# A chunked recurrence and a feed-forward block on one core: another fixed order of the first part, and four units whose scores come from the split form

## The chip, the cores and the metric

The kernel runs on one core of one Trainium2 chip. The metric is the device time of one execution in microseconds (us). The kernel before was run three times: 340.52, 343.04 and 342.12 us, a median of 342.12 us.

## The reference, cut to what matters

Four sequences of 768 tokens and 8 heads go through a linear recurrence, computed in chunks of 32 tokens. Its output (3072 tokens by 256) goes through a feed-forward block of width 2048 with a softplus between two matrix products. All of it is float32.

```python
log_a = np.log(np.clip(a, 1e-06, 1.0))
for c in range(nc):
    cum = np.cumsum(la, axis=-1)
    L = np.exp(cum[:, :, :, None] - cum[:, :, None, :]) * causal
    M = np.einsum('bhin,bhjn->bhij', Cc, Bc) * L
    y[:, :, sl] = (np.einsum('bhij,bhjd->bhid', M, xc)
                   + np.einsum('bhin,bhnd->bhid', Cc, state) * np.exp(cum)[:, :, :, None])
    state = decay_full * state + np.sum(Bx, axis=2)
...
h = x @ w_in
g = np.maximum(h, 0.0) + np.log1p(np.exp(-np.abs(h)))
out = g @ w_out
```

## The kernel before, in words

The recurrence is cut into 24 units of 128 tokens by 8 heads, six units for each sequence. Unit `i` goes through these steps (the letter in brackets is its word in the order):

- `decays` (D, L340): one affine select on POOL spreads the decay factors into `rm`, 128x1024.
- `score` (S, L378): the products of B and C, two 128x512 tiles `sp`, one for each group of four heads. There are two forms. A unit below `FIRST` (L30) is loaded with 576 KB from the array `fst`, in which C already lies apart by heads, and each tile is one plain float32 product over 64 rows (L386; L127 for units 0 to 7). A unit from `FIRST` on is loaded with 768 KB from the array `un`, and its tiles are four fp32r products of 256 columns (L391). These need `split_unit` first (L238): for `c_all` and for `b_rows` one copy on ACT (L247) and one scalar_tensor_tensor on DVE (L248), and two DMAs that put the halves of `c_all` into `c_rows` (L254). `c_rows` exists once, so one unit's DMAs wait until the scores of the unit before are done.
- `weigh` (M): two DVE products `m<-sp,rm`. `scale_b` (B) and `scale_c` (C) scale B and C by decays.
- `update` (U): products `zp` on PE, then `state` on DVE. `spread` (T) and `read` (R) bring the state before into `yp`; `within` (I) adds the unit's own 16 products.
- `grow` (G): two DVE products `y<-yp,gg`, one for each group of heads, then a copy to `xh` on ACT; `rest` (X): `xl<-y,xh` on DVE. `xh` and `xl` are the high and low parts of the block's input. `gg` is loaded from DRAM by `load_growth` (L225), 2 DMAs for three units (so `gg6` serves units 6 and 7).

The feed-forward block works on six pieces `j` of 512 tokens and 16 slices `k` of its width. `first` (F j.k) is six products `hp` of 512 columns (three for each half of the 256 inputs: high by high, low by high, high by low). `parts_of` (P) is a softplus `e` and a cast `gh` on ACT and a subtraction `gl` on DVE. `second` (Z j.k) is six products into two accumulators: `acc<-gh,woh`, `acc<-gl,woh`, `acc<-gh,wol` for each. The weights come in 16 loads (w0 to w15, 512 KB each, four buffers `wraw`) and are taken apart by `split_stages` (W, L522): one op on ACT, a shift and two scalar_tensor_tensor `w<-wraw,w` on DVE, a cast on ACT, and the subtraction `wil` or `wol` on DVE. Even steps make `wih`/`wil`, odd steps `woh`/`wol`. The fourth stage of a W is the last that reads its `wraw`, so the load that takes this buffer next waits for it.

**What sets the order.** All loads are issued on SP, one after the other, and each waits there until its buffer is free; the loads behind it wait too. For the first part (units 0 to 7, slices 0.0 to 0.11 and 1.0 to 1.7) the string `ORDER` (L53 to L68) lists every step by hand, and each engine keeps to it; these instructions all have the line L127 in the profile. A word of a staged step stands once for each of its stages: of W1 (stage 4 is the second scalar_tensor_tensor), of G6 (stage 1 is the two `y`), of P0.3 (stage 3 is `gl`). `warm` words put unused products on PE. What comes behind (units 8 to 23, the rest of the block, L761 on) is placed by a scheduler; unit 8's values go in at step `U_STEP[0]` = 20, and `prefetch` loads unit `i + 2` one step after unit `i`'s scores.

Of the kernel before, what the change touches and what calls it, by code (L numbers as in the profile page):

```python
# [26 lines left out]
NFT = DFF // P  # L27
TOK = NB * S
HEAD = 4
FIRST = 12  # L30
GU = 3
U_X = 0
U_B = U_X + DM
# [17 lines left out]


ORDER = """  # L53
warm1 warm7 la kc hc0 kb un0 w0 loga hc1 loga un1 gb ft0 lr hc2 un2 fr0 ft0 S0 w2 fr0 hc3 D0 fr0 un3 gq0 un4
fr0 w1 D1 W0 gq2 M0 w4 gq0 fr2 M0 S1 gq2 D3 fr2 C1 I0 logr M1 ft2 logr B0 B1 growth U0 C2 U1 U0 W0 fr2
growth T1 B2 fr2 gd U1 ft2 U2 M1 un5 D2 U2 R1 W2 G0 S3 G0 C3 W0 S2 T3 M3 I1 warm3 T2 W0 w6 M2 W0 M3 R3 D4 M2
I3 G1 R2 S4 G1 X0 C4 W0 gg3 I2 warm2 X1 W4 B3 D5 M4 G2 H0 C5 M4 U3 H1 W2 G2 U3 W2 S5 warm4 X2 T4 W2 w3 G3 W2
B4 R4 un6 M5 G3 I4 W2 U4 D6 G4 W1 U4 H2 G4 M5 H3 X3 X4 F0.0 T5 W4 F0.1 W1 P0.0 W4 R5 P0.1 W1 F0.2 P0.0 W4 I5
P0.1 w5 W1 F0.3 W4 D7 w7 G5 S6 warm2 W1 un7 G5 gg6 P0.2 W4 X5 W6 F0.4 M6 P0.2 W6 M6 F0.5 P0.0 W1 P0.3 I6 W6
W3 Z0.0 B6 P0.3 W6 w8 P0.1 U6 W6 U6 C7 Z0.1 W3 W6 P0.4 G6 S7 W5 T7 W3 G6 P0.2 R7 P0.4 F0.6 X6 P0.5 M7 P0.5  # L60
W3 F0.7 w10 M7 W3 P0.3 I7 W3 P0.6 G7 W7 Z0.2 W5 G7 P0.4 X7 P0.7 Z0.3 W5 P0.6 P0.5 W5 P0.7 F1.0 w12 W7 W5
P0.6 F1.1 P1.0 W5 W7 W8 Z0.4 P0.7 P1.1 W7 P1.0 F1.2 w14 W8 B7 W7 W8 W7 Z0.5 P1.2 P1.0 W10 W8 F1.3 P1.1 w9
W10 W8 P1.1 Z0.6 W8 P1.3 W10 W14 F1.4 P1.2 W10 w11 P1.2 W10 Z0.7 W14 P1.4 W10 W14 W9 F1.5 P1.3 W9 W14 F1.6
P1.5 w13 P1.3 W14 W9 F1.7 P1.6 W14 W9 W11 F0.8 w15 W11 W9 W11 F0.9 W9 W11 W13 F0.10 K0 W13 W13 W11 F0.11 W13
W11 W13 Z1.0 W15 W13 W15 W12 U7 Z1.1 W15 P1.4 W12 P1.4 P1.5 Z1.2 W12 P1.7 P1.5 P1.6 W15 Z1.3 P0.9 P1.6 W15
W12 P1.7 Z1.4 U7 W15 P0.11 P1.7 W12 Z1.5 P0.9 W12 P0.10 P0.9 P0.11 Z1.6 P0.8 P0.11 P0.10 Z1.7 P0.10 P0.8 K1
P0.8 zero
"""  # L68
HALF = NFT // 2
AHEAD = 20  # L70
# [34 lines left out]
def recurrence_then_ffn(ctx: ExitStack, tc: tile.TileContext, fst, un, at, al, w_in, w_out, const, outT):  # L105
# [28 lines left out]
    def load(out, in_):  # L134

        tc.keep_in_program_order(nc.sync.dma_start(out, in_))  # L136
# [73 lines left out]
    def load_unit(i):  # L210
# [4 lines left out]
        un_s[i] = p3.tile([P, U_END], F32, tag="un", name=f"un{i}")  # L215
        if i < FIRST:
            load(un_s[i][:, :F_END], fst[i])
        else:
            load(un_s[i], un[i - FIRST])

# [17 lines left out]
    def split_unit(i):  # L238
        if i < FIRST:
            return  # L240
        t = un_s[i]
        b_rows = p2.tile([P, NQ, P], F32R, tag="b_rows", name=f"b_rows{i}")

        def split(out, j):
            raw = t[:, U_S + j * NQ * P : U_S + (j + 1) * NQ * P].rearrange("p (q t) -> p q t", q=NQ)
            g, be = (kb[:, C_GB + v : C_GB + v + 1] for v in (2 * j, 2 * j + 1))
            A.activation(out, raw, AF.Copy, scale=be)  # L247
            V.scalar_tensor_tensor(out, raw, g, out.bitcast(F32), op0=ALU.mult, op1=ALU.add)  # L248

        c_all = p2.tile([P, NQ, P], F32R, tag="c_all", name=f"c_all{i}")  # L250
        split(c_all, 1)
        for e in range(2):
            rows = slice(64 * e, 64 * e + 64)
            load(c_rows[rows, :, e].bitcast(F32), c_all[rows].bitcast(F32))  # L254
        split(b_rows, 0)
        st[i] = b_rows
# [121 lines left out]
    def score(i, g):  # L378
        sp = mid[i]["sp", g] = ps.tile([P, 512], F32, tag="ps", name=f"sp{i}_{g}")
        if i < FIRST:  # L380
            rows = slice(64 * g, 64 * g + 64)
# [452 lines left out]
```

## Time and profile before

| | |
|---|---|
| three runs | 340.52, 343.04, 342.12 us (median 342.12) |
| profiled execution | 340.56 us, of which the span of the profile is 338.8 us |
| busy, share of the span | PE 328.7 us (97%), DVE 202.8 (60%), ACT 171.7 (51%), POOL 39.3 (12%) |
| TensorE clock granted | full speed in all 40 slices |
| DMA | 35.01 MB, mean 103 GB/s |

A row of the page's fifth part, or of the view by lines, names line, engine, operation, output and inputs, the count, busy time and the mean ns of one, and the idle time of its engine just before with what ended it. The chain of waits gives start, length, engine and product of each piece of the chain that ended last. In a timeline, an entry gives start, length, engine, line, operation and, in brackets, how long the engine stood idle before it and for what. The sixth part of the page gives the KB of each DMA and the time from issue to landing.

### The profile page before, as it was taken

Reading aid. Unit: us, or ns where it says so; the run is one execution under the profiler, and the core shown is the slowest. Engines: PE = TensorE matmul, PEld = TensorE weight load, DVE = VectorE, ACT = ScalarE, POOL = GpSimd, SP = SyncE. Lnnn points to the kernel's source line nnn. Section 1 sums busy time; section 2 is a strip of 40 time slices with the busy share of each in tenths; the row PEclk is TensorE's granted clock in tenths of the full one; section 3 lists DMA queues with packets and bytes.
Section 4 is the critical chain, followed back from the end, with each engine's and each line's share of the span. In section 5 each row is a group of like instructions: output and inputs, shape, how many; then the busy total and the mean of one; then the engine's idle time right before and its main releaser. Section 6 shows DMA issues by size and latency. Waiting matters only on the chain.

```text
span 338.8 us, 5271 instructions
## 1 busy us (share of the span) xinstructions
PE 328.7 (97%) x2047; PEld 249.4 (74%) x2047; DVE 202.8 (60%) x394; ACT 171.7 (51%) x319; POOL 39.3 (12%) x32
## 2 busy tenths in 40 slices
PE   8789998999999999999999999999999999999995
PEld 4446657887666678778778778778778778888885
DVE  0899989996946444864765464777474342232242
ACT  4845666875715435445445455445445244444450
POOL 2434510000111010110112010111010000000000
PEclk9999999999999999999999999999999999999999
DMA  7964533573032205416434205443203100010001
GB/s 233 396 228 138 220 106 104 188 259 120 3 98 114 93 0 189 133 39 186 126 61 141 95 0 188 122 106 99 94 2 93 33 0 0 2 55 8 2 0 62
DMA packets 19376, 35.01 MB, mean 103 GB/s; under 512 B 1432, under 2 KB 10136, under 8 KB 19352
## 3 DMA queue, kind: packets, MB, share of 16 engines
q1 hardware_dynamic: 19352, 34.68, 31.5%
q8 instruction: 16, 0.26, 0.3%
q14 instruction: 8, 0.07, 0.1%
HBM read 28.28 MB, written 3.24 MB: 93 GB/s over the span
## 4 chain that ended last, share of the span: by engine, by line
PE 86%; DVE 6%; DMA 5%; SPq 1%; issue 1%; ACT 0%
PE hp L563 32%; PE acc L642 32%; PE hp L127 6%; PE acc L127 6%; PE yp L466 3%; DMA gg<-gd 3%; DMA head_in_l<-in_fst 2%; PE yp L450 2%; PE sp L391 2%; DVE m L127 1%; DVE w L127 1%; PE sp L386 1%; SPq L136 1%; PE zp L416 1%; PE end L127 1%
## 5 line engine op out<-in xcount | busy, mean ns | idle before, releaser
L603 DVE TENSOR_TENSOR gl<-e,gh 128x512 fp32r<-128x512 f32 x76 | 55.7, 734 | 61.3 <-ACT gh L597 61.1
L597 ACT CAST gh<-e 128x512 fp32r<-128x512 f32 x76 | 47.1, 620 | 61.1 <-PE acc L642 60.3
L591 ACT ACTIVATE e<-hp 128x512 f32<-128x512 f32 x76 | 45.1, 596 | 42.4 <-DVE gl L603 38.5
L563 PE MATMUL hp<-xh,wih 128*128 128x512 f32 x152 | 61.3, 405 | 0.0
L642 PE MATMUL acc<-gl,woh 128*128 128x512 f32 x155 | 60.6, 391 | 0.0
L642 PE MATMUL acc<-gh,wol 128*128 128x512 f32 x155 | 60.5, 391 | 0.0
L642 PE MATMUL acc<-gh,woh 128*128 128x512 f32 x155 | 59.6, 391 | 0.0
L563 PE MATMUL hp<-xl,wih 128*128 128x512 f32 x152 | 59.5, 392 | 0.0
L563 PE MATMUL hp<-xh,wil 128*128 128x512 f32 x152 | 59.3, 391 | 0.0
L345 POOL TENSOR_SCALAR_AFFINE_SELECT rm<-fc 128x1024 f32<-128x1024 f32 x16 | 23.8, 1487 | 187.7 <-DVE m L402 167.8
L563 PEld LDWEIGHTS hp<-xh,wih 128*128 128x128 f32 x152 | 28.5, 188 | 10.7 <-issue 3.1
L642 PEld LDWEIGHTS acc<-gh,woh 128*128 128x128 f32 x155 | 29.1, 188 | 6.8 <-issue 0.8
L642 PEld LDWEIGHTS acc<-gh,wol 128*128 128x128 f32 x155 | 29.1, 188 | 6.2
L642 PEld LDWEIGHTS acc<-gl,woh 128*128 128x128 f32 x155 | 29.1, 188 | 6.1 <-issue 0.2
L563 PEld LDWEIGHTS hp<-xh,wil 128*128 128x128 f32 x152 | 28.5, 188 | 6.3
L563 PEld LDWEIGHTS hp<-xl,wih 128*128 128x128 f32 x152 | 28.6, 188 | 5.1
L402 DVE TENSOR_TENSOR m<-sp,rm 128x512 f32<-128x512 f32 x32 | 20.9, 685 | 7.9 <-PE sp L391 6.3
L127 DVE SCALAR_TENSOR_TENSOR w<-wraw,w 128x512 int32<-128x512 int32 x32 | 23.1, 729 | 0.2
L127 PE MATMUL hp<-xh,wih 128*128 128x512 f32 (+1 forms) x48 | 17.7, 368 | 2.0 <-DVE m L127 1.4
L127 PE MATMUL hp<-xl,wih 128*128 128x512 f32 (+1 forms) x48 | 17.0, 354 | 0.0
L127 PE MATMUL hp<-xh,wil 128*128 128x512 f32 (+1 forms) x48 | 17.0, 354 | 0.0
L127 POOL TENSOR_SCALAR_AFFINE_SELECT rm<-fc 128x1024 f32<-128x1024 f32 x8 | 14.0, 1764 | 20.8 <-DVE m L127 15.0
(109 smaller groups left out, 409.6 us busy)
## 6 DMA issues: line engine op xcount, KB each, us to landing
un<-in_un SPq DMA_DIRECT2D x12, 768.0 KB, 4.4
un<-in_fst SPq DMA_DIRECT2D x8, 576.0 KB, 6.1
wraw<-in_w_in SPq DMA_DIRECT2D x8, 512.0 KB, 3.4
wraw<-in_w_out SPq DMA_DIRECT2D x8, 512.0 KB, 5.2
c_rows<-c_all SPq DMA_DIRECT2D x24, 128.0 KB, 2.4
out_t<-o SPq DMA_DIRECT2D x11, 256.0 KB
gg<-gd SPq DMA_DIRECT2D x14, 192.0 KB
head_in_l<-in_fst SPq DMA_DIRECT2D x4, 320.0 KB, 6.2
```

What stands on the lines that cost most here:

```text
L127: return lambda *a, **k: tc.keep_in_program_order(f(*a, **k))
L136: tc.keep_in_program_order(nc.sync.dma_start(out, in_))
L345: Pl.affine_select(out=rm.rearrange("p h c i -> p (h c) i"), in_=fc[:, u].rearrange("p h c -> p (h c)").unsqueeze(2).broadcast_to([P, NH * ...
L391: PE.matmul(sp[:, 2 * v * P : 2 * (v + 1) * P], b_rows[:, q], c_rows[:, q].rearrange("p e t -> p (e t)"), start=True, stop=True,)
L402: V.tensor_tensor(mid[i]["m"][:, 4 * g : 4 * g + 4].rearrange("p h t -> p (h t)"), mid[i].pop(("sp", g)), mid[i]["rm"][:, 4 * g : 4 * g + ...
L450: PE.matmul(yp[q // 2][out], tb[rows].rearrange("p e d -> p (e d)"), cc[rows].rearrange("p c i -> p (c i)"), start=True, stop=False,)
L466: PE.matmul(yp[g][32 * hh : 32 * hh + 32], un_s[i][:, U_X + h * D : U_X + (h + 1) * D], m[:, h, :], start=u == 0, stop=True,)
L563: PE.matmul(h[:, c0:c1], w[:, c, fs], x[:, c, c0:c1], start=i == 0, stop=i == 5)
L591: A.activation(e, h, AF.Softplus)
L597: A.copy(gh, e)
L603: V.tensor_tensor(gl, e, gh.bitcast(F32), op=ALU.subtract)
L642: PE.matmul(acc[:, c0:c1], wo[v, k // HK][:, k % HK, es], g[:, c0:c1], start=start and i == 0, stop=stop and i == 2,)
```

## The change: what it does

`FIRST` goes from 12 to 8, and `ORDER` is another arrangement. The lines behind `ORDER` have numbers lower by one in the changed kernel.

```diff
@@ -27,7 +27,7 @@
-FIRST = 12
+FIRST = 8
@@ -51,20 +51,19 @@
 ORDER = """
-P0.1 w5 W1 F0.3 W4 D7 w7 G5 S6 warm2 W1 un7 G5 gg6 P0.2 W4 X5 W6 F0.4 M6 P0.2 W6 M6 F0.5 P0.0 W1 P0.3 I6 W6
...
+S6 G4 T5 W4 G4 R5 X4 W6 F0.4 W1 M6 D7 I5 M6 F0.5 G5 W1 G5 I6 w7 P0.0 W1 un7 X5 P0.3 W1 gg6 P0.3 W6 Z0.0 B6
...
 """
```

The words are the same apart from `warm`: 19 warming products become 14. With `FIRST` = 8, units 8 to 11 are loaded from `un` and take `split_unit` and the L391 form (L390 in the changed kernel). The loads on SP keep their order word for word up to gg9. From unit 12 on, and from Z0.2 to Z1.3, PE has the same instructions in the same order.

The first place is DVE around the fourth stage of W1 (the second `w1<-wraw1,w1`), which frees the buffer of w7; un7 and gg6 stand behind w7 on SP. Before:

```order
L127 TENSOR_SCALAR w1_455<-w1_455 128x512
L127 SCALAR_TENSOR_TENSOR w4_363<-wraw4_164,w4_363 128x512
L127 SCALAR_TENSOR_TENSOR w1_455<-wraw1_153,w1_455 128x512
L127 SCALAR_TENSOR_TENSOR w4_363<-wraw4_164,w4_363 128x512
L127 SCALAR_TENSOR_TENSOR w1_455<-wraw1_153,w1_455 128x512
L127 TENSOR_TENSOR y5_540<-yp5_0_498,gg3_348 128x128
L127 TENSOR_TENSOR y5_540<-yp5_1_499,gg3_348 128x128
L127 TENSOR_TENSOR wil_79<-w4_363,wih_78 128x2x256
L127 TENSOR_TENSOR xl_1_467<-y5_540,xh_1_466 128x2x128
L127 TENSOR_TENSOR m6_570<-sp6_0_543,rm6_450 128x512
L127 TENSOR_SCALAR w6_561<-w6_561 128x512
L127 TENSOR_TENSOR m6_570<-sp6_1_545,rm6_450 128x512
```

And now:

```order
L126 TENSOR_TENSOR y4_515<-yp4_0_481,gg3_325 128x128
L126 TENSOR_TENSOR y4_515<-yp4_1_482,gg3_325 128x128
L126 TENSOR_TENSOR tb5_518<-state4_476,kb_77 128x64
L126 TENSOR_TENSOR wil_79<-w4_398,wih_78 128x2x256
L126 TENSOR_TENSOR xl_1_522<-y4_515,xh_1_521 128x2x128
L126 SCALAR_TENSOR_TENSOR w1_312<-wraw1_155,w1_312 128x512
L126 TENSOR_TENSOR m6_541<-sp6_0_511,rm6_489 128x512
L126 TENSOR_TENSOR m6_541<-sp6_1_513,rm6_489 128x512
L126 TENSOR_TENSOR y5_561<-yp5_0_524,gg3_325 128x128
L126 TENSOR_TENSOR y5_561<-yp5_1_525,gg3_325 128x128
L126 SCALAR_TENSOR_TENSOR w1_312<-wraw1_155,w1_312 128x512
L126 TENSOR_TENSOR gl0_0_578<-e0_0_439,gh0_0_458 128x512
```

W1's fourth stage comes behind the two products `m6`, the two `y5` and the `wil` of w4, which stood behind it; nothing that stood ahead of it went behind it.

The second place is DVE between the products `y6`, which need `gg6`, and the `wol` of w3, which the third product of Z0.2 needs. Before:

```order
L127 TENSOR_TENSOR y6_641<-yp6_1_589,gg6_554 128x128
L127 TENSOR_TENSOR tb7_650<-state6_624,kb_77 128x64
L127 SCALAR_TENSOR_TENSOR w3_599<-wraw3_417,w3_599 128x512
L127 TENSOR_TENSOR gl0_2_654<-e0_2_557,gh0_2_572 128x512
L127 TENSOR_TENSOR xl_1_467<-y6_641,xh_1_466 128x2x128
L127 TENSOR_TENSOR m7_674<-sp7_0_644,rm7_536 128x512
L127 SCALAR_TENSOR_TENSOR w3_599<-wraw3_417,w3_599 128x512
L127 TENSOR_TENSOR m7_674<-sp7_1_646,rm7_536 128x512
L127 TENSOR_TENSOR gl0_3_690<-e0_3_586,gh0_3_611 128x512
L127 TENSOR_TENSOR wol0_81<-w3_599,woh0_80 128x512
L127 TENSOR_TENSOR y7_703<-yp7_0_656,gg6_554 128x128
L127 TENSOR_TENSOR y7_703<-yp7_1_657,gg6_554 128x128
```

And now:

```order
L126 TENSOR_TENSOR y6_659<-yp6_1_567,gg6_587 128x128
L126 TENSOR_TENSOR m7_662<-sp7_0_640,rm7_543 128x512
L126 TENSOR_SCALAR w5_655<-w5_655 128x512
L126 TENSOR_TENSOR m7_662<-sp7_1_642,rm7_543 128x512
L126 TENSOR_TENSOR xl_1_522<-y6_659,xh_1_521 128x2x128
L126 TENSOR_TENSOR wol0_81<-w3_603,woh0_80 128x512
L126 SCALAR_TENSOR_TENSOR w5_655<-wraw5_491,w5_655 128x512
L126 TENSOR_TENSOR y7_702<-yp7_0_665,gg6_587 128x128
L126 TENSOR_TENSOR y7_702<-yp7_1_666,gg6_587 128x128
L126 TENSOR_TENSOR gl0_3_705<-e0_3_584,gh0_3_590 128x512
L126 SCALAR_TENSOR_TENSOR w5_655<-wraw5_491,w5_655 128x512
L126 TENSOR_TENSOR xl_1_522<-y7_702,xh_1_521 128x2x128
```

The subtraction `gl0_3` stood just ahead of the `wol` of w3; it now comes four rows behind it. Ahead of the `wol` the second product `y6` is nearer to it: the `tb7`, two `w3` and `gl0_2` went ahead of `y6`.

The third place is PE where unit 8's scores come, among the products of Z1.7 and Z1.4 to Z1.6. Before:

```order
L127 MATMUL acc0_1_944<-gh1_7_1003,woh0_80 128x512
L563 MATMUL hp0_12_1069<-xh_0_272,wih_78 128x512
L563 MATMUL hp0_12_1069<-xl_0_273,wih_78 128x512
L386 MATMUL sp8_0_1084<-un8_1062 128x512
L386 MATMUL sp8_1_1088<-un8_1062 128x512
L563 MATMUL hp0_13_1095<-xh_0_272,wih_78 128x512
L563 MATMUL hp0_13_1095<-xl_0_273,wih_78 128x512
L127 MATMUL acc0_1_944<-gl1_7_1016,woh0_80 128x512
L127 MATMUL acc0_1_944<-gh1_7_1003,wol0_81 128x512
L127 MATMUL acc1_1_945<-gh1_7_1003,woh0_80 128x512
L127 MATMUL acc1_1_945<-gl1_7_1016,woh0_80 128x512
L127 MATMUL acc1_1_945<-gh1_7_1003,wol0_81 128x512
```

And now:

```order
L126 MATMUL acc1_1_937<-gl1_4_966,woh0_80 128x512
L126 MATMUL acc1_1_937<-gh1_4_953,wol0_81 128x512
L390 MATMUL sp8_0_1085<-c_rows_86,b_rows8_1075 128x256 x2
L126 MATMUL acc0_1_936<-gh1_5_977,woh0_80 128x512
L126 MATMUL acc0_1_936<-gl1_5_981,woh0_80 128x512
L126 MATMUL acc0_1_936<-gh1_5_977,wol0_81 128x512
L126 MATMUL acc1_1_937<-gh1_5_977,woh0_80 128x512
L126 MATMUL acc1_1_937<-gl1_5_981,woh0_80 128x512
L126 MATMUL acc1_1_937<-gh1_5_977,wol0_81 128x512
L126 MATMUL acc0_1_936<-gh1_6_983,woh0_80 128x512
L390 MATMUL sp8_1_1090<-c_rows_86,b_rows8_1075 128x256 x2
L126 MATMUL acc0_1_936<-gl1_6_995,woh0_80 128x512
```

The scores of unit 8 now come between Z1.4 and Z1.5 and within Z1.6, in four products of 256 columns that read `c_rows` and `b_rows8`. On SP there stood, around the same time:

```order
L136 DMA un8_1062<-in_fst 128x1152
L136 DMA un9_1064<-in_fst 128x1152
L136 DMA gg9_1066<-gd_84 128x1x384 x2
L136 DMA un10_1138<-in_fst 128x1152
L136 DMA un11_1207<-in_fst 128x1152
L136 DMA un12_1309<-in_un 128x1536
L136 DMA gg12_1311<-gd_84 128x1x384 x2
```

And now:

```order
L135 DMA un8_1055<-in_un 128x1536
L135 DMA un9_1057<-in_un 128x1536
L135 DMA gg9_1059<-gd_84 128x1x384 x2
L135 DMA c_rows_86<-c_all8_1076 64x4x128 x2
L135 DMA un10_1141<-in_un 128x1536
L135 DMA c_rows_86<-c_all9_1157 64x4x128 x2
L135 DMA un11_1220<-in_un 128x1536
L135 DMA c_rows_86<-c_all10_1263 64x4x128 x2
```

The two DMAs into `c_rows` of units 8 to 10 come between the loads of units 9 to 12. On ACT the copies for `c_all` and `b_rows` of units 8 and 9, and that for `c_all10`, come ahead of the softplus `e0_8`.

More of the change, by code (lines that the diff above doesn't have):

```diff
@@ L53 @@
 ORDER = """
[L54 to L58, printed above, removed]
@@ L59 @@
-P0.1 w5 W1 F0.3 W4 D7 w7 G5 S6 warm2 W1 un7 G5 gg6 P0.2 W4 X5 W6 F0.4 M6 P0.2 W6 M6 F0.5 P0.0 W1 P0.3 I6 W6
[L60 to L67, printed above, removed]
+warm1 warm7 la kc hc0 kb un0 w0 loga hc1 loga un1 gb ft0 lr hc2 fr0 un2 ft0 S0 fr0 w2 hc3 D0 fr0 un3 gq0 fr0
+un4 W0 w1 gq2 D1 gq0 M0 w4 S1 gq2 M0 C1 fr2 D2 logr M1 I0 logr ft2 fr2 growth C2 B0 S2 W0 growth M1 ft2 gd
@@ new lines @@
+D3 G0 U0 un5 M2 W2 fr2 S3 U0 G0 M2 fr2 T1 W0 R1 X0 C3 I1 warm3 W0 w6 G1 W0 B1 B2 G1 U1 W2 U2 warm3 W0 X1 W1
+U1 H0 M3 gg3 U2 H1 W2 T3 M3 R3 T2 W2 I3 R2 D4 w3 W2 un6 I2 C4 G2 G3 S4 G2 W2 G3 X2 W4 H2 X3 B3 H3 M4 D5 C5
+F0.0 M4 F0.1 P0.0 B4 U3 W4 P0.1 F0.2 W1 P0.0 U3 U4 W4 S5 P0.1 T4 U4 P0.2 W4 R4 P0.2 D6 w5 M5 F0.3 W4 M5 I4
+S6 G4 T5 W4 G4 R5 X4 W6 F0.4 W1 M6 D7 I5 M6 F0.5 G5 W1 G5 I6 w7 P0.0 W1 un7 X5 P0.3 W1 gg6 P0.3 W6 Z0.0 B6
+W3 W6 P0.1 U6 W6 P0.4 Z0.1 w8 U6 P0.4 W3 T7 W6 W3 P0.2 C7 S7 W6 P0.5 W3 F0.6 W5 w10 G6 M7 W3 R7 G6 W5 F0.7
@@ new lines @@
+M7 P0.5 X6 W3 I7 W5 W7 Z0.2 G7 P0.3 G7 W5 P0.6 Z0.3 w12 X7 P0.6 P0.4 W5 F1.0 P0.5 P0.7 W5 P0.7 W7 F1.1 P0.6
+P1.0 W8 W7 Z0.4 P1.1 P0.7 W7 P1.0 F1.2 w14 W8 B7 W7 P1.0 Z0.5 W7 P1.2 W8 W10 F1.3 P1.1 W8 w9 P1.1 W8 Z0.6
+W10 P1.3 W8 W10 W14 F1.4 P1.2 W10 w11 P1.2 Z0.7 W10 W14 P1.4 W10 P1.3 F1.5 W14 W9 P1.3 F1.6 W9 P1.5 W14 w13
+W9 W14 F1.7 P1.6 W9 w15 W14 W9 F0.8 W12 W9 F0.9 W12 W11 W12 W11 F0.10 W12 W11 K0 F0.11 W11 W12 W11 Z1.0 W12
+W11 W13 U7 P1.4 W13 Z1.1 U7 W15 P1.4 W13 P1.7 Z1.2 P1.5 W15 W13 P1.5 P1.6 Z1.3 W15 P0.8 W13 P1.6 P1.7 Z1.4
@@ L68 @@
+W15 P0.11 W13 W15 P1.7 Z1.5 P0.8 W15 P0.9 P0.8 P0.11 Z1.6 P0.10 P0.11 P0.9 Z1.7 P0.9 P0.10 K1 P0.10 zero
 """
```

## The prediction

> **What bounds the kernel now.** I read the page's busy shares first, then the chain of waits, then the timelines of DVE and SP where the chain leaves PE. The view by windows gives the busy time of each engine in a stretch of 10 us (PE, PEld, DVE, ACT and POOL, each with its count of instructions):
>
> ```profile
> span 338.8 us, 5271 instructions
> PE 328.7 (97%) x2047; PEld 249.4 (74%) x2047; DVE 202.8 (60%) x394; ACT 171.7 (51%) x319; POOL 39.3 (12%) x32
> ...
> 20.00:30.00 10.00, 8.11 (x92) 4.43 (x90) 9.92 (x23) 4.19 (x14) 3.69 (x3) 1.00 0.31 90
> 30.00:40.00 10.00, 9.78 (x76) 7.46 (x77) 9.60 (x22) 7.71 (x14) 6.78 (x3) 1.00 0.69 271
> ...
> 50.00:60.00 10.00, 9.15 (x53) 7.13 (x46) 9.99 (x20) 6.73 (x13) 1.35 (x1) 1.00 0.33 109
> 60.00:70.00 10.00, 10.00 (x46) 8.27 (x45) 9.72 (x18) 8.28 (x14) 0.00 (x0) 1.00 0.52 160
> ...
> 80.00:90.00 10.00, 10.00 (x50) 7.06 (x48) 7.72 (x17) 6.79 (x14) 0.00 (x0) 1.00 0.17 56
> ```
>
> So there are two regimes. From 60 us on PE is full: every microsecond taken from its products is won, if nothing else opens a gap. Up to 60 us DVE is nearly full, and PE has gaps. The chain says where the last of them closes:
>
> ```profile
> 36.53 9.29 DMA gg<-gd
> ...
> 49.01 0.60 DVE m L127
> 49.61 0.60 DVE gl L127
> 50.21 1.68 DVE wol L127
> 51.94 2.57 PE acc L127 x10
> ```
>
> The second half of `gg6` lands at 36.53 + 9.29 = 45.82 us, DVE then works without a pause to the `wol` of w3, and PE's third product of Z0.2 waits for that. From 51.94 us on the chain is PE (its DVE and DMA pieces all lie ahead of that). Thus the time is the moment at which this `wol` is done, plus the work of PE behind it.
>
> **The change, part one: PE's products for the scores of units 8 to 11.** The chain shows one unit's scores in each form, and what stands behind them:
>
> ```profile
> 104.21 1.06 PE sp L386 x4
> 105.27 1.58 PE hp L563 x6
> ...
> 142.55 0.47 PE sp L391 x4
> 143.02 0.69 PE acc L642 x3
> ...
> 145.09 0.68 PE acc L642 x3
> 145.77 1.36 PE hp L563 x6
> ```
>
> Six products `hp` take 1.36 us, but 1.58 behind the plain scores: PE pays 0.22 for going from 64 rows to 128. So a unit costs 1.06 + 0.22 = 1.28 us in the plain form. In the split form it is 0.47, and the three `acc` behind take 0.69 for 0.68: 0.48. Four units give 4 x 0.80 = 3.2 us. In the changed order `yp` of these units goes to and fro between its two kinds of product (two L449, four L465, two L449, four L465, where L450 stood together), some three more changes of form; at half of the 0.22, an estimate, that takes back 0.3. **-2.9 us**, with -3.2 and -2.5 (three changes at the full 0.22) as its ends.
>
> **Part two: the fourth stage of W1.** Here are DVE's and then SP's timelines around it:
>
> ```profile
> 32.46 2.48 DVE L127 SCALAR_TENSOR_TENSOR w<-wraw,w 128x512 int32<-128x512 int32 x4
> 35.04 0.51 DVE L127 TENSOR_TENSOR y<-yp,gg 128x128 f32<-128x128 f32 x2
> 35.55 1.07 DVE L127 TENSOR_TENSOR wil<-w,wih 128x512 fp32r<-128x512 f32 x1
> ...
> 45.85 0.29 DVE L127 TENSOR_TENSOR y<-yp,gg 128x128 f32<-128x128 f32 x1 [1.36 <-DMA gg<-gd]
> 46.06 0.21 DVE L127 TENSOR_TENSOR tb<-state,kb 128x64 f32<-128x64 f32 x1
> 46.19 0.69 DVE L127 SCALAR_TENSOR_TENSOR w<-wraw,w 128x512 int32<-128x512 int32 x1
> ...
> 50.13 1.75 DVE L127 TENSOR_TENSOR wol<-w,woh 128x512 fp32r<-128x512 f32 x1
> ```
>
> ```profile
> 34.41 0.98 SPq L136 DMA_DIRECT2D wraw<-in_w_out  x2
> 35.48 0.42 SPq L136 DMA_DIRECT2D un<-in_fst  x1
> 35.95 1.12 SPq L136 DMA_DIRECT2D gg<-gd  x2
> ```
>
> W1's fourth stage is the last of the four at 32.46 and ends at 34.94. At once SP issues w7 (the second of the two loads), then un7, then both halves of `gg6`: these are released by that one DVE instruction. The last lands 45.82 - 34.94 = 10.9 us later, and DVE stands idle for 1.36 us waiting for it. In the changed order five DVE instructions come ahead of this stage and none goes behind: two `m6`, the `wil` of w4, two `y5`. A DVE product of this size takes 0.60 us from start to start (49.01, 49.61, 50.21 above), the two `y` 0.51: 3 x 0.60 + 0.51 = 2.3. That gives 37.25 at the earliest. Two things can add to it. The `m6` now have to wait for their `rm`, which POOL made late:
>
> ```profile
> 31.19 4.90 POOL L127 TENSOR_SCALAR_AFFINE_SELECT rm<-fc 128x1024 f32<-128x1024 f32 x1 [4.72 <-DVE m L127]
> ```
>
> It ended at 36.09; DVE would now ask for it at about 34.9 (34.94 less the last stage, plus `wil`), a wait of up to 1.2. And `wil` can be held up, as at 35.55 (1.07 for 0.60) or as `wol` was (1.75): up to 1.15 more. So 37.25 to 39.6; I take 38.4, with the wait for `rm` and no further hold-up. Then `gg6` lands at 38.4 + 10.9 = 49.3 instead of 45.82.
>
> Behind it less is left to do before the `wol` of w3. From the second `y6` to the start of `wol` it was 50.13 - 45.85 = 4.28 us; `tb7` (0.13), two `w` (1.2) and `gl0_2` (0.6) now come ahead of `y6`, `gl0_3` (0.6) behind the `wol`, and a shift of w5 comes in (0.33, an estimate: a shift is half the size of a product in time, two of them take 0.67 by the rows next to 32.46): 2.08. So `wol` ends at 49.3 + 2.1 + 1.75 = 53.1 instead of 51.88: 1.25 later. Behind it come a `w` (0.6), two `y7` (0.4) and only then `gl0_3` (0.68): it is done 1.7 us after `wol`. PE needs it five products after the one that `wol` releases, and ten took 2.57: 5 x 0.26 = 1.3. PE waits 0.4 more. **+1.65 us.** From there PE's order is the same up to Z1.3 and PE has no gap, so that this delay stays to the end.
>
> Its ends: with W1 at 39.6 it is 2.85. In the other direction, the wait for `gg6` could vanish: DVE was ready for the second `y6` at 45.85 - 1.36 = 44.49, which is 9.55 behind W1's end; less the 2.3 that moved ahead of W1, plus the 1.93 that moved ahead of `y6`, that is 9.2. With W1 at 37.25, `y6` could run at 46.4 and `wol` end at 50.3, 1.6 earlier: with the 0.4 a gain of 1.2. So -1.2 to +2.85.
>
> [...]
>
> **Part three: the new work of units 8 to 11.** Each unit now has two copies on ACT, two instructions on DVE and two DMAs, and 768 KB to load instead of 576:
>
> ```profile
> L248 DVE SCALAR_TENSOR_TENSOR b_rows<-un,kb,b_rows 128x512 fp32r<-128x512 f32 x12 | 12.0, 1000 | 0.2
> L248 DVE SCALAR_TENSOR_TENSOR c_all<-un,kb,c_all 128x512 fp32r<-128x512 f32 x12 | 10.0, 837 | 1.5 <-ACT c_all L247 1.5
> L591 ACT ACTIVATE e<-hp 128x512 f32<-128x512 f32 x76 | 45.1, 596 | 42.4 <-DVE gl L603 38.5 <-PE hp L563 3.5
> L247 ACT ACTIVATE c_all<-un,kb 128x512 fp32r<-128x512 f32 x12 | 8.7, 724 | 12.0 <-DMA un<-in_un 11.9
> un<-in_un SPq DMA_DIRECT2D x12, 768.0 KB, 4.4
> c_rows<-c_all SPq DMA_DIRECT2D x24, 128.0 KB, 2.4
> ```
>
> That is 4 x (1.00 + 0.84) = 7.4 us of DVE and 4 x 1.44 = 5.8 of ACT between about 75 and 115 us. From 80 to 90 us DVE is busy 7.72 of 10 and ACT 6.79, so that 2.3 and 3.2 are free there, and one unit in about 10 us brings 1.84 and 1.44. It fits; if it did not, up to 7.4 us would be exposed. What counts is when. The scores of unit 8 stand behind Z1.0 to Z1.4 and six `hp`, and Z1.0 starts at 76.27:
>
> ```profile
> 76.27 1.36 PE acc L127 x6
> ...
> 71.07 0.93 SPq L136 DMA_DIRECT2D un<-in_fst  x2
> 77.94 15.54 SPq L136 DMA_DIRECT2D un<-in_fst  x2
> ...
> 83.71 0.29 DVE L360 TENSOR_TENSOR bp<-un,ft 128x128 f32<-128x128 f32 x1 [2.26 <-DMA un<-in_fst]
> ```
>
> Six blocks of 1.36 put them at 84.4 (all of this moves with the first part). The load at 71.07 lands 4.4 later at 75.5; `c_all` 0.72 and 0.84; two issues 0.93 (as the two at 71.07) and a landing 2.4: 80.4. Some 4 us are left for queueing on ACT and DVE: hidden. The second scores `sp8_1`, nine products later at 86.5, need a free PSUM buffer, and so the softplus `e0_8` on ACT, which now stands behind `c_all10`, which needs unit 10's load. That load went out at 77.94 and was there at 83.7; it is now behind the `c_rows` DMAs of unit 8 (77.1 by this sum, with queueing 78.5, and two issues), so out at 79.5 and there at 84 to 85.3. Then 0.72 and 0.6 (`e`): 85.3 to 86.6, against 86.5. Just covered. Queued behind unit 10's load on SP are the `c_rows` of unit 9 and unit 11's load, and behind `c_all10` on ACT `e0_8` and `gh1_7`, which Z1.7 waits for. Without the cover it costs the 1.6 by which the load goes out later less what is covered, or 3 with the 1.9 that `c_all` (0.72), `e` (0.60) and a `gh`, put at the same as `e`, take on ACT. I take **+0.5**, ends 0 and 3.
>
> The five `warm` products that go stand in the first 40 us, where PE is not full (8.11 of 10 from 20 to 30 us, with DVE at 9.92): what they took comes back as idle time. Nothing.
>
> **The sum** is -2.9 + 1.65 + 0.5 = -0.75 us. The profiled execution of before took 340.56 us (span 338.8 and 1.76 around it), so it would be 339.8; the median of the three runs is 342.12, and against that the forecast is **341.4 us**: no change that can be told. About 1%, 3.4 us, is what a measurement of this kernel can tell from no change.
>
> **Rivals.** *B, the first part keeps its pace*: W1's stage ends by 37.25 and `gg6` comes in time, or is quicker than 10.9. For it: w5, which went out at 34.41 just ahead of it, goes out much earlier now; against it: DVE has no gap in front of W1 (9.60 of 10). Then part two is between 0 and -1.2 and the time 342.12 - 2.9 - 0.6 = 338.6.
>
> *C, slower: the wait for `gg6` grows.* If W1's stage ends at 39.6, because `wil` is blocked beside the late `rm`, `gg6` lands at 50.5; part two is +2.85, and if unit 10's load then also holds up `e0_8` by 3 us, the sum is -2.9 + 2.85 + 3 = +3: 345.1. Every tenth that W1 ends later costs a tenth, so that the change becomes a loss from 38.4 + 0.75 = 39.15 on. For it: 1.36 us of waiting for `gg` there already, and an `rm` that took 4.90; against it: POOL waited 4.72 for an `m` ahead of that `rm`, and the order now has D6 ahead of both stages of M5 instead of between them.
>
> *D, the saved products are not won*: PE's scores are shorter but PE waits elsewhere (ACT's `e`, `gl` or the landing of `c_rows` at units 9 to 11, one buffer for all of them), so that the 2.9 come back as gaps, and only the first part tells: 342.12 + 1.65 = 343.8. For it: four loads now wait on one SP queue behind `c_rows`; against it: the same chain serves units 12 to 23, and PE's slices show no gap there:
>
> ```profile
> PE   8789998999999999999999999999999999999995
> ```
>
> **How the numbers follow.** The forecast 0.52, B 0.25, C 0.13, D 0.10. The range runs from 337.6 (B with all its low ends is -3.2 - 1.2 = -4.4, so 337.7) to 344.9 (C); the likeliest case's own is 339.8 to 342.8. Faster by over 1% means under 338.7: half of B and a little of the rest, 0.17. Slower by over 1% means over 345.5: part of C, 0.10. The rest, 0.73, lies within 1%.
>
> **What the changed profile would show.** Right: the `sp` of units 8 to 11 take 0.47 for 1.06; the fourth stage of W1 ends near 38.4 and the second `y6` waits some 2 to 3 us for `gg`; the `wol` of w3 ends near 53, and PE's wait in Z0.2 goes 1.2 later, with a wait for `gl` behind it; Z1.0 starts at about 78. Wrong: the `wol` of w3 done by 52, no `gg` in the chain (then B); a PE gap ahead of `sp8_1` or `sp9` longer than 1 us (then C or D).

## The result, and the profile after

The changed kernel takes 346.04 us (median of four runs, 345.43 to 347.26), the kernel before beside it on the same chip 341.32 us: a ratio of 1.0142, with a 95% interval of 1.0109 to 1.0175. The change costs 4.7 us; the forecast was 341.4 us. The profiled execution took 345.43 us, its span is 343.7 us, 4.9 more than before.

The page of the changed kernel starts with the span and the busy time:

```profile
span 343.7 us, 5292 instructions
PE 329.8 (96%) x2042; PEld 252.1 (73%) x2042; DVE 207.6 (60%) x402; ACT 175.9 (51%) x327; POOL 39.1 (11%) x32
...
PEclk9998998999999999999999999999999999999999
```

PE's granted clock, 9 tenths or more in every slice before, now falls to 8 tenths in two of the 40 slices (last row). The chain that ended last, in the first part, and then at the scores of unit 12, where PE's order is the same in both kernels:

```profile
20.74 7.00 DMA gg<-gd
...
44.62 8.97 DMA gg<-gd
53.96 2.93 PE hp L126 x6
56.89 0.60 PE yp L126 x16
57.48 3.02 PE acc L126 x12
...
138.88 0.47 PE sp L390 x4
```

The last `acc` of Z0.3 ends at 60.50 us (57.48 + 3.02); before, it was 54.51 (51.94 + 2.57). The first part thus ends 6.0 us late. Unit 12's scores come at 138.88 us, before at 134.00: the delay has shrunk by 1.1 us on the stretch where units 8 to 11 take the other form. The rest takes as long as before. So the change has two halves, +6.0 and -1.1, and both differ from the forecast (+1.65 and -2.4).

DVE's timeline shows what happened in the first half:

```profile
25.22 0.29 DVE L126 TENSOR_TENSOR y<-yp,gg 128x128 f32<-128x128 f32 x1 [0.95 <-DMA gg<-gd]
27.77 0.29 DVE L126 TENSOR_TENSOR y<-yp,gg 128x128 f32<-128x128 f32 x1 [2.26 <-DMA gg<-gd]
...
30.85 1.84 DVE L126 TENSOR_SCALAR w<-w 128x512 int32<-128x512 int32 x2
33.38 0.28 DVE L126 SCALAR_TENSOR_TENSOR state<-state,fr,zp 128x64 f32<-128x64 f32 x1 [0.69 <-PE zp L126]
...
41.45 1.62 DVE L126 SCALAR_TENSOR_TENSOR w<-wraw,w 128x512 int32<-128x512 int32 x1
...
51.17 0.29 DVE L126 TENSOR_TENSOR y<-yp,gg 128x128 f32<-128x128 f32 x1 [1.20 <-DMA gg<-gd]
53.61 0.29 DVE L126 TENSOR_TENSOR y<-yp,gg 128x128 f32<-128x128 f32 x1 [2.15 <-DMA gg<-gd]
...
55.68 1.75 DVE L126 TENSOR_TENSOR wol<-w,woh 128x512 fp32r<-128x512 f32 x1
...
58.36 0.68 DVE L126 TENSOR_TENSOR gl<-e,gh 128x512 fp32r<-128x512 f32 x1
```

The two `y3` come at 25 us and wait 0.95 + 2.26 = 3.2 us for `gg3`; before, they came at 28.00 and did not wait. The fourth stage of W1 ends at 41.45 + 1.62 = 43.07 us instead of 34.94. SP then issues w7, un7 and gg6:

```profile
35.48 7.99 SPq L135 DMA_DIRECT2D wraw<-in_w_out  x2
43.56 0.42 SPq L135 DMA_DIRECT2D un<-in_fst  x1
44.03 1.11 SPq L135 DMA_DIRECT2D gg<-gd  x2
```

`gg6` lands 10.5 us behind that stage (44.62 + 8.97 = 53.59), and DVE's wait for it is 1.20 + 2.15 = 3.35 us instead of 1.36. PE waits with it: F0.7's products start at 53.96, right behind the second `y6`, and take 2.93 us, where the same six took 1.4 before.

In the view by windows the granted clock stands third from the end; the share of the DMA engines and the GB/s follow. Here are four stretches of the changed kernel, and then two of the kernel before:

```profile
24.00:28.00 4.00, 1.81 (x6) 0.81 (x6) 0.80 (x5) 0.94 (x5) 0.27 (x1) 1.00 0.95 270
28.00:32.00 4.00, 3.29 (x18) 3.29 (x19) 4.00 (x10) 3.40 (x8) 1.14 (x1) 0.70 0.16 63
32.00:36.00 4.00, 4.00 (x40) 2.53 (x40) 2.96 (x7) 3.28 (x7) 0.41 (x1) 0.87 0.01 2
...
54.00:58.00 4.00, 4.00 (x25) 2.67 (x26) 4.00 (x7) 1.34 (x3) 1.34 (x1) 0.64 0.08 28
```

```profile
24.00:28.00 4.00, 3.84 (x28) 2.31 (x28) 3.92 (x10) 0.82 (x3) 1.34 (x1) 1.00 0.11 41
28.00:32.00 4.00, 3.29 (x49) 2.67 (x48) 4.00 (x14) 3.00 (x5) 0.81 (x1) 1.00 0.68 222
```

PE is busy 1.81 of 4 us from 24 to 28 us, and then gets 0.70 and 0.87 of its clock. The stretch from 54 to 58 us, in which F0.7's slow products lie, has 0.64. Before, the order had two and four warming products at 22 and 27 us and PE was busy 3.84 of 4.

In the second half, PE's timeline shows one gap; the chain leads to it:

```profile
92.25 0.51 PE L126 MATMUL acc<-gl,woh 128*128 128x512 f32 x1 [0.89 <-DVE gl L126]
```

```profile
76.94 7.07 DMA un<-in_un
...
90.26 0.73 DVE b_rows L247
...
91.59 0.61 DVE gl L126
```

It is Z1.5's second product, whose `gl` stands in DVE's queue behind the new `c_all` and `b_rows` of unit 9. The chain begins at the load of unit 8, which lands 7.07 us after its issue; the forecast had allowed 4.4.

### The profile page after: what moved, and what is told of

Read it like the earlier page. It is cut to its first block, busy times and chain, and to the rows that moved or that the text cites. A ratio compares the mean times of both kernels' runs of the same rounds, so it can differ in the third digit from the quotient of the medians.

```text
span 343.7 us, 5292 instructions
## 1 busy us (share of the span) xinstructions
PE 329.8 (96%) x2042; PEld 252.1 (73%) x2042; DVE 207.6 (60%) x402; ACT 175.9 (51%) x327; POOL 39.1 (11%) x32
## 4 chain that ended last, share of the span: by engine, by line
PE 80%; DMA 10%; DVE 5%; SPq 2%; ACT 1%; issue 1%; ACTq 0%
PE acc L641 31%; PE hp L562 31%; DMA gg<-gd 5%; PE hp L126 5%; PE acc L126 4%; PE yp L465 3%; PE sp L390 2%; DMA un<-in_un 2%; DMA gd<-lr 2%; SPq L135 2%; PE yp L449 2%; DMA head_in_h<-in_fst 2%; DVE w L126 2%; PE zp L415 1%; PE end L126 1%
## 5 line engine op out<-in xcount | busy, mean ns | idle before, releaser
L344 POOL TENSOR_SCALAR_AFFINE_SELECT rm<-fc 128x1024 f32<-128x1024 f32 x16 | 26.1, 1631 | 188.0 <-DVE m L401 172.9
L246 ACT ACTIVATE c_all<-un,kb 128x512 fp32r<-128x512 f32 x16 | 11.6, 724 | 20.7 <-DMA un<-in_un 20.7
L126 PE MATMUL hp<-xh,wih 128*128 128x512 f32 (+1 forms) x48 | 19.0, 396 | 2.2 <-DVE y L126 2.2
L126 PE MATMUL hp<-xh,wil 128*128 128x512 f32 (+1 forms) x48 | 18.3, 382 | 2.6 <-DVE wil L126 2.6
L126 PE MATMUL hp<-xl,wih 128*128 128x512 f32 (+1 forms) x48 | 18.2, 380 | 0.0
```

Of the source, the lines that this page charges most:

```text
L126: return lambda *a, **k: tc.keep_in_program_order(f(*a, **k))
L344: Pl.affine_select(out=rm.rearrange("p h c i -> p (h c) i"), in_=fc[:, u].rearrange("p h c -> p (h c)").unsqueeze(2).broadcast_to([P, NH * ...
```

## The experiments

The theory that they test (A): the new order of the first part loses the time, through its waits for `gg`; the split form gains. The rival (B): the split form of units 8 to 11 loses it. All differences are to the kernel before as run beside them, by the ratio. Single executions of one kernel differ by some 2 us either way (the kernel before, 339.7 to 344.9), so the medians judge, and a profile only tells where.

| run | median us | before beside it | ratio (95%) |
|---|---|---|---|
| old order, units 8 to 11 split | 344.67 | 342.64 | 1.0077 (1.0047 to 1.0107) |
| new order, units 8 to 11 plain | 349.93 | 342.64 | 1.0236 (1.0171 to 1.0301) |
| gg6 early | 342.76 | 342.64 | 1.0007 (0.9970 to 1.0045) |
| y3 later | 345.41 | 342.64 | 1.0093 (1.0050 to 1.0135) |
| zero adds ahead of F0.7 | 346.88 | 341.97 | 1.0166 (1.0121 to 1.0211) |
| before, gg6 early | 340.18 | 341.97 | 0.9931 (0.9899 to 0.9964) |
| old order, split, un10 ahead | 344.61 | 341.97 | 1.0102 (1.0059 to 1.0146) |
| gg6 early, un10 ahead | 345.01 | 341.97 | 1.0113 (1.0067 to 1.0158) |
| warm8 ahead of H2 | 345.35 | 342.22 | 1.0105 (1.0061 to 1.0148) |
| gg6 early, warm8 | 341.50 | 342.22 | 0.9982 (0.9961 to 1.0002) |
| before, gg6 early, units 10 and 11 split | 338.32 | 342.22 | 0.9924 (0.9888 to 0.9961) |
| before, gg6 early, units 8 and 9 split | 339.99 | 342.22 | 0.9962 (0.9925 to 0.9998) |

**The two halves of the change, each alone.**

```diff
 kernel before
-FIRST = 12
+FIRST = 8
```

> The old order of the first part, with units 8 to 11 in the split form. Theory A (the new order loses the time in its waits for gg, and the split form gains): 338 to 340.5 us, 1 to 3 below the kernel before, with Z0.3 ending at 54.5 us as before and the sp rows of units 8 to 11 at 0.47 us. Rival B (the split form of units 8 to 11 loses the time, by its chain of loads, copies and DMAs): 343 us or more, with gaps of PE behind Z1.3.

Measured: 344.67 us, 0.8% above the kernel before. A fell in its second half, and B's time is right: with the old order the split form is a loss. The chain of this kernel shows why:

```profile
80.37 7.35 DMA un<-in_un
...
87.83 0.10 ACT c_all L247
...
88.45 0.44 ACT e L127
...
91.11 1.22 PE hp L563 x2
92.33 0.85 PE sp L391 x4
```

Unit 10's load is issued at 80.37 us, behind unit 8's DMAs into `c_rows`. The copy `c_all10` on ACT waits for it, with a softplus `e`, the cast `woh` and the `gh` of Z1.7 behind it in ACT's queue. In PE's timeline the step to Z1.7's first product takes 2.9 us instead of 0.23, and smaller ones follow; Z1.7 ends 5.2 us behind its time before, Z1.6 only 1.3. This was the stall of the prediction's part three, at a little more than rival C's price (3.9 us for 3).

```diff
 changed kernel
-FIRST = 8
+FIRST = 12
```

> The new order of the first part, with units 8 to 11 in the plain form as before. Theory A: Z0.3 ends 6.0 us later than before (60.5 instead of 54.5 us) and the whole takes 347 to 348 us, more than the changed kernel. Rival B: within 2 us of the kernel before.

Measured: 349.93 us, 2.4% above, more than A said. In its profile Z0.3 ends 5.0 us late, where A said 6.0, and 2.4 more are lost behind Z1.3. There the plain scores of units 8 and 9 stand apart, one tile at a time, those of unit 11 together:

```profile
90.17 1.05 PE sp L385 x2
91.23 1.58 PE acc L126 x6
92.81 1.05 PE sp L385 x2
...
111.78 1.06 PE sp L385 x4
```

One tile alone takes 1.05 us, two behind one another take 1.06 together, and the 0.22 behind them is paid once or twice. So these two units cost some 1.26 us more each than unit 11 (2 x 1.27 against 1.28), 2.5 in all, which accounts for the 2.4. By the ratios the split form is worth 0.94 points, some 3.2 us, under the new order, with intervals that just overlap; under the old one it costs 0.77 points, 2.6 us.

In the view by windows of this profile PE's granted clock is 1.00 in every stretch of 4 us from 20 to 40 us and from 50 to 58 us, so the new order loses its 5.0 us in the first part without a dip of the clock there.

**gg6 early.** The load of `gg6` needs only the buffer that `y2` frees; what held it up was its place on SP, behind w7.

```diff
 changed kernel, ORDER
-... I2 C4 G2 G3 S4 ... W1 un7 X5 P0.3 W1 gg6 P0.3 ...
+... I2 C4 G2 gg6 G3 S4 ... W1 un7 X5 P0.3 W1 P0.3 ...
```

> The changed kernel with the load of gg6 issued on SP behind un6 and ahead of w5, so that it does not wait for the fourth stage of W1. Theory A: DVE's waits of 1.20 and 2.15 us at y6 go; the wol of w3 ends 3.3 us earlier (54.1 instead of 57.4), PE has no 2 us gap ahead of F0.7 and does its six products in 1.5 instead of 2.9 us; 341.5 to 343 us, 3 to 4.5 below the changed kernel. Rival B: the time stays within 1 us of the changed kernel, since the gap only moves to units 8 to 11.

Measured: 342.76 us, the same as before: 1.35 points of the ratio, some 4.6 us, are gone from 1.42. A holds. DVE's timeline has no wait at `y6`, and the `wol` of w3 is done at 51.5 instead of 57.4:

```profile
48.53 0.47 DVE L126 TENSOR_TENSOR y<-yp,gg 128x128 f32<-128x128 f32 x2
...
50.80 0.68 DVE L126 TENSOR_TENSOR wol<-w,woh 128x512 fp32r<-128x512 f32 x1
```

```diff
 kernel before, ORDER
-... M4 G2 H0 C5 ... un7 G5 gg6 P0.2 ...
+... M4 G2 gg6 H0 C5 ... un7 G5 P0.2 ...
```

> The kernel before with the load of gg6 issued right behind the first stage of G2, so that it does not wait for the fourth stage of W1. Theory A: DVE's wait of 1.36 us at y6 goes, the wol of w3 ends 1.4 us earlier and Z0.3 ends 0.9 to 1.4 us earlier; 0.9 to 1.4 us below the kernel before. Rival B: the wol of w3 was going to wait for DVE's queue anyway, or the earlier load slows w3 and un6: no change within 0.5 us.

Measured: 340.18 us, 0.69 points below the kernel before, some 2.4 us and more than A said. The wait of 1.36 us that the kernel before has there is the same thing. This version beats both kernels.

The two runs belong together: with `gg6` early in both, the changed kernel is still 0.76 points, some 2.6 us, above the old one (1.0007 against 0.9931, intervals apart). So of the 1.42 points that the change costs, the longer wait for `gg6` carries about half; the other half stays when that wait is gone from both, and is as large as the loss by the split form under the old order (0.77). That it is the same loss is not shown.

**The two y3 later.**

```diff
 changed kernel, ORDER
-I2 C4 G2 G3 S4 G2 W2 G3 X2 W4 H2 X3 B3 H3 M4 D5 C5 F0.0 M4 F0.1 P0.0 B4 U3 W4 P0.1
+I2 C4 G2 S4 G2 W2 X2 W4 M4 D5 C5 H2 M4 H3 B4 W4 G3 G3 X3 B3 F0.0 F0.1 P0.0 U3 P0.1
```

> The changed kernel with the two y3 put behind the two m4, bp4 and the wil of w2 on DVE, about where they stood before (H2, H3, B3, U3 and F0.0 move a little with them). Theory A: DVE's waits of 0.95 and 2.26 us for gg3 shrink to under 0.6; the fourth stage of W1 ends 2.5 to 3.5 us earlier (about 40 instead of 43.1), gg6 lands as much earlier, and the whole is 2 to 4 us below the changed kernel (342 to 344). Rival B: W1 ends earlier, but the end does not move by more than 1 us, because gg6 or PE's free buffers hold it up as before.

Measured: 345.41 us, 0.5 points below the changed kernel, with intervals that overlap; W1's fourth stage ended at 42.9 instead of 43.1. Counted from the issue of `gd` on SP (13.85 us here, 12.98 in the changed kernel) it is 1.0 us sooner, where A said 2.5 to 3.5. A fell here: the wait for `gg3` became 1.41 us, and others came in its place:

```profile
29.66 0.29 DVE L126 TENSOR_TENSOR y<-yp,gg 128x128 f32<-128x128 f32 x1 [1.41 <-DMA gg<-gd]
...
32.80 0.28 DVE L126 SCALAR_TENSOR_TENSOR state<-state,fr,zp 128x64 f32<-128x64 f32 x1 [1.42 <-PE zp L126]
```

So moving `y3` back by itself does not undo it. `gg3`'s landing counts for what comes behind it (`xl3`, H, F, `zp3`), wherever `y3` stands; whether an earlier or a quicker `gg3` would was not tried (its 192 KB take 7.0 us in the changed kernel's chain, the 768 KB of a unit 5.0 by the median).

**The clock.** First, PE's idle 2.0 us ahead of F0.7 is filled with six products that add zeros to an accumulator.

```diff
 changed kernel, ORDER
-R7 G6 W5 F0.7
+R7 G6 W5 idle6 F0.7
 the new word
+    def add_nothing(n):
+        for _ in range(n):
+            PE.matmul(accs[0][0][:32]..., some, some..., start=False, stop=False)
```

> The changed kernel with six products on PE just ahead of F0.7, which add zeros to the first accumulator of Z0 and fill PE's idle 2.0 us there (51.95 to 53.96 in the changed kernel). Theory A, that the granted clock falls after idle time (0.83 in the stretch from 50 to 60 us, and F0.7's six products took 2.93 us for 1.6): F0.7 takes 1.6 to 1.8 us, Z0.3 ends 1 to 1.4 us earlier relative to y6, and the whole is 1 to 1.4 us below the changed kernel. Rival B, that F0.7 was held up by its operands: F0.7 takes 2.9 us as before and the whole stays the same.

Measured: 346.88 us, no gain. In the profile both halves of the answer stand side by side:

```profile
52.44 1.47 PE L126 MATMUL acc<-some 128*32 128x512 bf16 x6
54.50 0.50 PE L126 MATMUL hp<-xh,wih 128*128 128x512 f32 x1 [0.59 <-DVE y L126]
54.84 0.39 PE L126 MATMUL hp<-xl,wih 128*128 128x512 f32 x1
...
58.03 0.50 PE L126 MATMUL acc<-gh,wol 128*128 128x512 f32 x1 [0.63 <-DVE wol L126]
```

The six products of F0.7 now go at 0.23 to 0.34 us apart, and the clock is 1.00 from 50 to 60 us, so it was the clock and not their operands. But then Z0.2 waits 0.63 us for the `wol` of w3: part of what the slow clock took would have been waited for anyway. The second edit fills the gap ahead of H2, where the old order had warming products.

```diff
 changed kernel, ORDER (and the same with gg6 early)
-W2 G3 X2 W4 H2 X3
+W2 G3 X2 W4 warm8 H2 X3
```

> The changed kernel with eight warming products just ahead of H2, where its order lost those of the order before. Theory A, that PE's idle time from 24 to 28.7 us lowers the granted clock (0.70 from 28 to 32 and 0.87 from 32 to 36 us) and so delays what DVE waits for: the clock is 1.00 there, H2 to F0.1 take 1.3 to 2 us less, and the whole is 0.5 to 1.5 us below the changed kernel. Rival B: the clock comes back, but DVE's chain through the two loads gg3 and gg6 is what counts, and the whole stays within 0.5 us.

> The changed kernel with gg6 loaded early and the eight warming products ahead of H2. Theory A: with gg6 out of the way a lowered clock in the stretch from 20 to 36 us is what is left of the loss in the first part; Z0.3 ends within 1 us of the kernel before, in every run, and the median is 340.5 to 342, 0.5 to 2 us below gg6 early alone. Rival B: the same as gg6 early alone (342.8), within 0.5 us.

Measured: 345.35 us against 346.04 (0.4 points less, within the intervals), and with gg6 early 341.50 against 342.76 (0.25 points less, again within them). The clock comes back in both profiles; the row is that of the first:

```profile
32.00:36.00 4.00, 4.00 (x50) 2.51 (x50) 3.84 (x9) 3.43 (x7) 0.67 (x2) 1.00 0.06 20
```

Both go A's way, and W1's fourth stage ends at 41.9 us in both instead of 43.1, but the gain in the time is not shown beyond doubt. How much is at stake differs by execution: of gg6 early, one profile had 1.00 from 28 to 36 us, and that of the run with gg6 early and un10 ahead, which has the same first part, only half of the clock:

```profile
32.00:36.00 4.00, 4.00 (x25) 3.60 (x25) 2.47 (x5) 2.31 (x4) 1.55 (x1) 0.50 0.17 60
```

There Z0.3 ended 4.2 us later than in the first; 1.7 of them stood there ahead of the dip already, since `gg3` landed at 29.4 instead of 27.7 us.

**Unit 10's load.**

```diff
 kernel before with FIRST = 8 (and the changed kernel with gg6 early)
-        if i + 2 < NB * NU:
+        if EARLY < i < NB * NU - 2:
             plan(s + 1, prefetch, i + 2)
-    for i in range(EARLY, EARLY + 2):
+    for i in range(EARLY, EARLY + 3):
         prefetch(i)
```

> The old order with units 8 to 11 in the split form, and the load of unit 10 issued on SP ahead of the two DMAs of unit 8 into c_rows instead of behind them. Theory A, that the 3.6 us which PE lost at Z1.7 come from the copy c_all10 on ACT, which waits 4.8 us for unit 10's load with e0_8 behind it: the load goes out some 1.2 us earlier, ACT's wait falls to about 3.5 us and the gap to about 2.4 us; 1 to 1.5 us below the run with the old order and units 8 to 11 split. Rival B, that the gap comes from the DMAs into c_rows of unit 8 or from DVE's queue: the gap stays at 3.6 us or grows, since those DMAs go out later.

> The changed kernel with both edits: gg6 loaded early, and unit 10's load ahead of unit 8's DMAs into c_rows. Theory A: the first part as with gg6 early alone (Z0.3 within 1 us of the kernel before), no gap of PE above 0.5 us behind Z1.3, so 340 to 342 us, 0.5 to 1.5 below gg6 early alone. Rival B: no difference to gg6 early alone (within 0.5 us).

Measured: 344.61 us, the same as without the edit, and 345.01 us, 1.1 points above gg6 early alone. A fell in both: the two DMAs into `c_rows` now come behind 768 KB, and it is they that land late. The chain of the first of the two:

```profile
82.02 7.45 DMA c_rows<-c_all
...
89.58 0.10 ACT c_all L247
...
90.21 0.58 ACT e L127
```

They take 7.45 us (6.91 in the other run), where the page has a median of 2.4. Then two units at a time, on the kernel before with gg6 early:

```diff
-FIRST = 12
+FIRST = 10                             # units 10 and 11
...
+PLAIN = (0, 1, 2, 3, 4, 5, 6, 7, 10, 11)      # or: units 8 and 9
-        if i < FIRST:
+        if i in PLAIN:
```

> The kernel before with gg6 early, and units 10 and 11 alone in the split form (8 and 9 plain). Theory A: the copy c_all10 on ACT waits for unit 10's load with e0_9, e0_8 and gh1_7 behind it, so PE has a gap of 1 to 3 us at Z1.7 and the gain of two units (1.1 to 1.5 us) is lost: 340 to 342 us. Rival B: no gap, 338.7 to 339.2.

> The kernel before with gg6 early, and units 8 and 9 alone in the split form (10 and 11 plain). Theory A: no copy on ACT waits for unit 10's load, so PE has no gap above 0.5 us behind Z1.3 and two units gain 1.1 to 1.5 us: 338.7 to 339.5, below the kernel before with gg6 early (340.2). Rival B, that the DMAs of units 8 and 9 into c_rows are what PE waits for: a gap as with all four units, 342 to 344.

Measured: 338.32 and 339.99 us, against 340.18 for none of the four: three ratios whose intervals overlap. In the profiles both have a gap, of some 1.8 us at Z1.6 and Z1.7 and of some 2.2 at Z1.5 and Z1.6. For units 10 and 11 the gap is as A said, though no `c_rows` DMA stands ahead of unit 10's load there: the copy `c_all10` waits 2.84 us for its 768 KB. The time is not as A said: 338.32 us lies below its 340 to 342, and below B's 338.7 to 339.2 too, so the medians do not show that this gap costs the gain of two units. For 8 and 9 A's rule "no copy on ACT, no gap" was wrong. Their chain:

```profile
78.36 0.67 SPq L138
...
79.78 6.40 DMA un<-in_fst
...
86.21 0.29 DVE bp L362
86.50 0.20 DVE cc L378
86.70 0.61 DVE gl L129
```

Unit 10's load is again issued behind the `c_rows` DMAs, and it is DVE's `bp10` and `cc10` that wait for it, ahead of the `gl` that PE needs. So in these profiles it is a DMA on the one queue that lands late, and whatever waits for it first on ACT or DVE passes it on. Whether an own buffer for unit 10 would end it was not tried.

## Why the prediction was wrong, point by point

**Part one** (-2.9 us for the scores). The `sp` of units 8 to 11 take 0.47 us for four, as forecast. From Z0.3 to unit 12's scores the changed kernel is 1.1 us shorter with a gap of 0.9 in it, so PE's own work fell by some 2.0 instead of 2.9. Counted from start to start of PE's products on this stretch, the `sp` take 1.99 us for 4.24 and the `yp` 5.13 for 4.84, both about as forecast (4 x 0.59 less, 0.3 more). What was mis-sized is the change of form, 4 x 0.22 = 0.88: what the `hp` and `acc` pay at such changes fell by some 0.4 only. Why is not shown; `zp` and `yp` stand between them in nine blocks now and in eight before.

**Part two** (+1.65 us; measured +6.0) is the step that failed, in its sentence on W1: "five DVE instructions come ahead of this stage and none goes behind ... That gives 37.25 at the earliest", with 39.6 as the latest. The count was right and the stage ended at 43.07. I had added up DVE's work ahead of it and taken over its idle time from the old order. But the new order also has `y3` some six instructions sooner, at 25 us, and `gg3`, issued at 20.00, lands at 27.7: 3.2 us of new waiting that no wait of before could show, since there `y3` came late enough. In all, DVE's waits up to this stage add up to 13.3 us, before to 8.9. I had followed the queue on SP for `gg6` and not for `gg3`, though both hang on it. The two shifts (1.84 us for 0.67) and the last stage itself (1.62 for 0.6) come on top with 2.2. These three are read from profiles, and the five DVE timelines of this order that cover them agree (1.6 to 3.7 us of waiting for `gg3`, 1.84 and 1.62 us in each, the stage at 41.7 to 45.9); what each is worth is not shown, and `y3` later, which took only a part of the first away, won 1.0 us at that stage. The next step, from W1's stage to `gg6` (10.9 us forecast, 10.5 measured) and to a longer wait at `y6`, held. Loading gg6 early takes 4.6 us off the changed kernel, which shows that this wait lies on its path; but 2.4 of them come off the kernel before as well, so about half of the 4.7 us is this step's.

What I said holds PE there, the `wol` of w3 alone, was incomplete: PE stopped earlier, at F0.7, which starts just behind the second `y6` (53.96 us behind 53.61 + 0.29 in the changed kernel). That the reason is the PSUM buffer that `y6` empties fits the order, but was only argued.

**Warming products** ("Nothing") were costed wrongly. The cover that I named, PE's idle time, is itself what came before the lower clock in the changed kernel (0.70, and 0.50 in another run). The price in the medians is 0.25 to 0.4 points, within the intervals, and the new order without a dip lost 5.0 us of the 6.0 all the same.

**Part three** (+0.5, ends 0 and 3): the gap is 0.9 us in the changed kernel, and Z1.7 loses 3.9 under the old order. The mechanism, unit 10's load behind `c_rows`, is that of the old order; in the changed kernel the gap hangs on the copies of unit 9 ahead of a `gl` and on unit 8's load. The runs with un10 ahead show that issuing unit 10's load earlier on the same queue is no repair.

**Rivals.** C was right in direction and place (W1's stage, then `gg6`), and its point of decision (39.15) was passed by 4 us. The rest of it did not come: the `wil` of w4 took 0.68 us, no `m6` waited for an `rm`, and unit 10's load held up nothing for 3 us in the changed kernel. The range left a time of 346.04 out, since its worst case was W1 at 39.6; its top, 344.9, lies even below C's own 345.1. What speaks for C's reason, a DVE instruction held up beside an `rm` on POOL, are rows of the profiles: in the kernel before, the `wol` of w3 takes 1.75 us beside an `rm` (49.74 to 51.35 us) where others of its size take 0.68; in the changed kernel it takes 1.75 again beside one (55.56 to 56.90), and the last stage of W1 1.62 beside another (41.26 to 42.54). No run tested that the one is the cause of the other, and of the 8.1 us by which W1 came later that stage's 1.0 is a small part.

## What to carry to other kernels

When a fixed order is rearranged, do not carry the idle times of the old trace over to the new queue: list each load with the time at which it can land at the earliest, and see which instruction now arrives before it, for every load and not only for the one that waits already. A load that is held up only by its place on the issuing queue is the first thing to move (here 0.7% for one word in the kernel before), while a big load moved ahead of a small urgent one can make that one late (here the `c_rows` DMAs behind 768 KB took 7.45 us in one run, by the median 2.4). When an edit takes a loss away, make the same edit to the kernel before: only what it does not gain there belongs to the change. Before filling products are taken out of PE's idle time, look at the granted clock behind it (here 0.70 from 28 to 32 us, behind 4 us with PE busy for 1.81).

## What the runs showed of the hardware that was not expected

- The two score tiles of a unit in the plain form, one from the upper 64 rows and one from the lower, run side by side when they come back to back: 1.06 us for both, in the kernel before and in the run with the new order and plain units, where one alone took 1.05. The price of the plain form therefore depended on whether the scheduler kept them together.
- A DMA of 128 KB into `c_rows` lands in 2.4 us by the median, and in 7.45 and 6.91 in the two runs where a unit's load of 768 KB stood ahead of it on SP. How the two share the way is not shown.
- With PE busy 1.81 of 4 us its granted clock fell to 0.70 and 0.87 for the next 8 us (in another execution 2.81 of 4, then 0.71 and 0.50), and with filling products ahead of the work (busy 3.80 of 4) it was 1.00. The waits of PE ahead of the dips are 2.58 us in the changed kernel, 2.94 in the run at 0.50, and 2.01 ahead of F0.7 (0.64 from 54 to 58 us). How long PE was idle does not tell it by itself: in the run with the new order and plain units PE was idle for 2.06 of the 4 us from 50 to 54 us, and the clock was 1.00 there and in the next 4 us; a wait of 1.65 us in front of `zp`, at about 19 us, stands ahead of 0.59 from 20 to 24 us with gg6 early and of 1.00 in the changed kernel. Why the same first part was hit in one execution and spared in another is not shown.
